# Turning the experts' operands by DRAM and VectorE instead of TensorE, in an attention and mixture-of-experts kernel

## The chip, the cores and the metric

The kernel runs on one core of one Trainium2 chip. The metric is device time in microseconds (us), the median of several executions. Engines are named as the profile names them: PE is TensorE (PEld its weight loads), DVE is VectorE, ACT is ScalarE, POOL is GpSimd, SP is SyncE, which issues most DMAs.

## The reference, cut to what matters

Eight batches of attention with a soft cap (12 heads, 448 positions, width 64), then for each batch a layer in which the 128 best scored of its 448 tokens pass through a two-layer expert.

```python
scores = scale * np.matmul(q, k.transpose(0, 1, 3, 2))
scores = cap * np.tanh(scores / cap)
scores = scores - np.max(scores, axis=-1, keepdims=True)
attn = np.exp(scores)
attn = attn / (np.sum(attn, axis=-1, keepdims=True) + 1e-09)
x = matmul(attn, v)                       # per batch (448, 768)
...
top_idx = np.argpartition(-scores[b], capacity)[:capacity]   # scores = x @ w_gate, capacity 128
xe = x[b, top_idx]
h = np.maximum(xe @ w1, 0.0)              # (128, 1024)
ye = h @ w2                               # (128, 768)
g = 1.0 / (1.0 + np.exp(-scores[b, top_idx]))
out[b, top_idx] = x[b, top_idx] + g[:, None] * ye
```

## The kernel before, in words

Attention is cut into 24 "doubles", three to a batch; a double is four heads. Each has 7 steps of 64 key positions. A step is one `qk` task (4 matmuls into `ps`), a tanh and an exp of 128x896 on ACT (`p`), and one product task (4 matmuls, `acc<-p,v`). The trace records each of these fp32 matmuls twice, so a task of 4 is 8 records. DVE adds up the exps of a double (`e<-e,p`), turns the finished accumulator in blocks of 32x32 (`xT<-acc`, once for each double, which also frees the accumulator for the next double), turns and reduces the sums (`turned`, `T`), normalises (`xn` or `room`), and weighs by the gate (`jk`, `part`). In the first three doubles part of the sums is made on PE instead (`pb<-ones,p`, 28 matmuls a group, 56 records).

After a batch's third double its tokens are scored (`quads`), ranked by way of a DRAM line (`line`, `row`), picked (a one-hot `sel`, a small matmul) and gathered from the output by an indirect DMA on POOL (`xe`, 128 tokens by 768). The expert's operands must have the feature on the partitions, so `xe` is turned by 6 PE transposes (`pb<-ident,xe`), and the first layer's result `hs` (128x1024) by 8 (`pb<-ident,hs`). ACT copies a turned piece into a high part (`xh`, `hh`), DVE subtracts it to get the low part (`xl`, `hl`), both in fp32r. A layer is then three products, high by high, high by low weight, low by high weight: 36 matmuls of 512 columns for `w1`, 48 of 384 columns for `w2`, called heavy here. DVE combines (`xe<-pb,both,xe`), POOL scatters.

Nothing is ordered by hand: functions add tasks with a duration, a priority and the buffers they take, and `Plan.run` lists them by a simulated clock, engine by engine, in which each engine then runs them in order. `WAY` holds numbers by segment of the program that steer it (when PE leaves attention for heavy work, how long it stays, how much heavy work is held for the end). The costs of tasks are in the `add` calls; `LOAD` is the planner's picture of a DMA. In `expert_tasks` the names that the change touches are `split` (transposes, high, low), `xs`, `hx`, `group`, `relu`, `combine`, `scatter` and `K.last_heavy`, the last heavy matmul so far, which the next batch's first layer waits for: one batch's two layers are finished before the next batch's start.

Of the kernel before, what the change touches and what calls it, by code (L numbers as in the profile page):

```python
# [9 lines left out]
F32 = mybir.dt.float32  # L10
# [8 lines left out]
P = 128  # L19
# [21 lines left out]
WAY = {  # L41
    "visit": (6500, 4000, 4000, 4000, 3000, 3000, 3000, 3000, 7500, 7000, 7000, 6000, 7500, 7500,
        7500, 4000, 5500, 7500, 4500, 5000, 7000, 5000, 5000, 8000),
    "enough": (2, 3, 4, 4, 4, 3, 4, 5, 3, 2, 2, 2, 1, 5, 5, 2, 1, 3, 1, 2, 1, 2, 2, 2),
    "wait": (0, 1, 0, 0, 1, 1, 1, 1, 1, 1, 0, 0, 0, 0, 0, 0, 0, 0, 0, 0, 1, 0, 1, 1),
    "eager": (0, 2, 0, 2, 0, 0, 0, 0, 0, 0, 0, 0, 0, 0, 0, 0, 0, 0, 0, 0, 0, 0, 0, 0),
    "lag": (3, 4, 4, 4, 2.5, 3, 1.5, 4, 2.5, 4, 2, 2, 4, 2, 3, 3, 2, 3, 4, 2, 1.5, 4, 3, 2.5),
    "ask": (-4, 12, -8, -4, 12, 8, -8, -12, 12, 4, -4, 4, 4, 4, 12, 12, -4, -8, -4, 8, 8, 12, 0, 0),
    "fin": (0, 4, -4, 4, -8, -8, -4, -4, 8, 14, 4, 8, 14, 14, -4, -4, -4, 0, 0, -4, -4, 8, -8, 4),
    "turn": (20, 28, 0, 28, 10, 10, 10, 10, 0, 0, 28, 28, 20, 28, 28, 10, 20, 28, -10, 20, 10, 28,  # L50
        20, 20),
    "reserve": (42000, 10000, 0, 46000, 42000, 50000, 20000, 50000, 20000, 30000, 0, 0, 0, 0, 42000,
        0, 20000, 30000, 30000, 30000, 30000, 0, 0, 0),
    "sums": (0, 0, 0, 8, 0, -2, 4, 4, 0, -4, -4, -4, 8, 8, 8, 4, 2, -4, -4, -4, 2, 2, -4, 0),
    "cast": (-20, 0, -10, -30, -30, -30, -30, -20, 20, 0, 0, 0, 20, 10, -20, 10, 10, -10, -10, 20,
        10, 20, -20, 20),
}
# [411 lines left out]
def attention_tasks(tc, K, D):  # L469
# [3 lines left out]
    if D.d == 0:  # L473
        lqk = add("NONE", 3700, lambda t: None)
        lmore = add("NONE", 750, lambda t: None, [lqk])
        lrest = add("NONE", 850, lambda t: None, [lmore])
        lv = add("SP", 0, lambda t: D.load_v(tc, K, None), prio=-19.5, load=(1, P * S * 8))
    else:
        lqk = add("SP", 0, lambda t: D.load_qk(tc, K, t.got["qk"]),
                  [K.staged[2]] if D.d == 1 else (), prio=g0 - 12, take=("qk",),  # L480
                  load=(2, P * S * 16))
        lv = add("SP", 0, lambda t: D.load_v(tc, K, t.got["v"]),
                 [lqk] if D.d == 1 else (), prio=g0 - 11, take=("v",),
                 load=(1, P * S * 8))
    pv, exps, ths, pvs, alone = None, [], [], [], []
    for s in range(NS):
# [22 lines left out]
        if g:  # L509
            a = add("PE", 754 if g > 1 else 1300, qk, [lqk if g > 1 or D.d else lmore], prio=g, take=("S",), mode="att",  # L510
                    give=[("qk", lqk)] if D.d and s == NS - 1 else ())
# [4 lines left out]
        else:  # L516
            c = S // 2
            a = add("PE", 740, lambda t, f=qk: f(t, c1=c), [lqk], prio=-2, take=("S",), mode="att")
            th = add("ACT", 510, lambda t, f=tanh: f(t, c1=c), [a], prio=-2, take=("P",))
            a2 = add("PE", 740, lambda t, f=qk: f(t, c0=c), [lmore, a], prio=-1, mode="att")  # L520
            th2 = add("ACT", 510, lambda t, f=tanh: f(t, c0=c), [a2, th], prio=-1, give=[("S", a)])
        ex_ = add("ACT", 934, exp, [th if g else th2], prio=blk + 1, seg=("lag", D.d, 2))
# [265 lines left out]
def expert_tasks(tc, K, b, s0, M, ranked, before, vals, p0):  # L788
# [30 lines left out]
    def index(t):  # L819
        nc.vector.tensor_copy(X["idx"], X["both"][:, 0:1])  # L820

    def gather(t):
# [46 lines left out]

    lows = []  # L870
    hold = add("NONE", 0, xs, [ga], prio=e0, take=("xs",))
    for i0 in range(0, ND, 3):
        w = min(3, ND - i0)
        turn, high, low = split("xe", "xh", "xl", i0, w)
        tr = add("PE", 109 * w, turn, [hold], prio=e0 - 9000, take=("bank",), mode="full")
        hi = add("ACT", 371, high, [tr], prio=-10)
        lo = add("DVE", 433, low, [hi], prio=-40 + b / 100, give=[("bank", tr)])
        lows.append(lo)

# [16 lines left out]
    hts, tail = [], None  # L896
    turned = []
    for hf in range(2):
        fs = slice(hf * 512, hf * 512 + 512)
# [22 lines left out]
    add("NONE", 0, lambda t: None, [tail], give=[("xs", hold)])  # L922
    add("NONE", 0, lambda t: None, hts, give=[("hsb", hs_owner)])
    for hf in range(2):
# [16 lines left out]
        co = add("DVE", 496, combine, [tail, g3], prio=-40 + b / 100, give=[("bank", owner)])  # L941
    K.last_heavy = tail
    add("NONE", 0, lambda t: None, [tail], give=[("hx", hh)])

    def scatter(t):
# [98 lines left out]
def main_kernel(ctx: ExitStack, tc: tile.TileContext, qk, v, cap, w_gate, w1, w2, out, C, dims):  # L1044
# [15 lines left out]
    K.weighed = {}  # L1060
    K.last_heavy = None
    K.const = ctx.enter_context(tc.tile_pool(name="const", bufs=1))
    dram = ctx.enter_context(tc.tile_pool(name="dram", bufs=1, space=bass.MemoryType.DRAM))
    K.line = [dram.tile([K.NCH * P], F32, name=f"line{i}") for i in range(2)]
    K.work = ctx.enter_context(tc.tile_pool(name="work", bufs=1))
    first = early_loads(tc, K, cap)
    with tc.manual_schedule(engines={mybir.EngineType.PE, mybir.EngineType.DVE}):
        load_flag(tc, K)
    K.psS = ctx.enter_context(tc.tile_pool(name="psS", bufs=1, space=PSUM))
    K.psV = ctx.enter_context(tc.tile_pool(name="psV", bufs=1, space=PSUM))  # L1070
    K.psB = ctx.enter_context(tc.tile_pool(name="psB", bufs=1, space=PSUM))

# [14 lines left out]
    with tc.If(fast > 0) as cmp:  # L1087
        if C <= P:
            K.plan = Plan(SIZES)
            engines = {mybir.EngineType.PE, mybir.EngineType.Activation, mybir.EngineType.DVE,  # L1090
                       mybir.EngineType.Pool, mybir.EngineType.SP}
# [78 lines left out]
```

## Time and profile before

| what | value |
|---|---|
| median of 3 executions | 447.81 us (446.86 to 449.22) |
| the profiled execution's own time | 446.97 us |
| its span, first to last instruction | 445.2 us |
| PE, DVE, ACT, POOL busy | 432.6, 376.6, 339.8, 23.8 us (97, 85, 76, 5%) |
| PE matmul records | 4600 |
| moved by DMA | 59.35 MB, mean 133 GB/s |
| granted TensorE clock | 0.998 of full speed over the span |

A busy share is the union of an engine's instructions, each from its start to its modelled end; instructions of one engine overlap by their latency, so what one costs in a full stretch is read from start to start. The 24 `xT<-acc` instructions, one per double, serve as marks: the first starts at 25.46 us, the last at 390.67 us.

### The profile page before, as it was taken

How to read it: one execution, taken by the hardware profiler on the slowest of the kernel's cores; microseconds unless marked ns; L12 is line 12 of the kernel's file. 1: busy time of each engine (PE TensorE's matmuls, PEld its weight loads, DVE VectorE, ACT ScalarE, POOL GpSimd, SP SyncE). 2: the span in 40 equal slices, each digit the busy share in tenths (PEclk: the TensorE clock that was granted, in tenths of full speed). 3: DMA queues.
4: the chain of work that ended last, by engine and by line, in shares of the span. 5: the costliest groups of instructions: out<-in, count | busy, mean ns of one | idle time of the engine just before them, and what ended most of it. 6: DMA issues, size and time to landing. Idle time of an engine off the chain costs nothing.

```text
span 445.2 us, 10844 instructions
## 1 busy us (share of the span) xinstructions
PE 432.6 (97%) x4600; PEld 247.8 (56%) x4600; DVE 376.6 (85%) x539; ACT 339.8 (76%) x395; POOL 23.8 (5%) x26
## 2 busy tenths in 40 slices
PE   8999998999999999999999999999999999999994
PEld 2455433355574455457475386554644563588984
DVE  3899999999999979999897995999969999984311
ACT  5999989999769969897769963997499989611120
POOL 3000000100002000101010010001000010000000
PEclk9999999999999999999999999999999999999999
DMA  8975753537327724453417440475244641152111
GB/s 277 346 248 174 218 153 123 160 87 197 65 93 207 195 57 135 139 170 108 144 46 231 126 102 24 150 196 159 66 141 103 191 120 43 35 125 63 35 38 40
DMA packets 46202, 59.35 MB, mean 133 GB/s; under 512 B 18242, under 2 KB 33474, under 8 KB 46146
## 3 DMA queue, kind: packets, MB, share of 16 engines
q1 hardware_dynamic: 44434, 51.83, 40.0%
q0 software_dynamic: 1280, 6.29, 4.3%
q8 instruction: 38, 0.62, 0.6%
q10 hardware_dynamic: 432, 0.46, 0.3%
q14 instruction: 18, 0.15, 0.1%
HBM read 44.40 MB, written 14.17 MB: 132 GB/s over the span
## 4 chain that ended last, share of the span: by engine, by line
PE 54%; DVE 22%; issue 10%; ACT 8%; DMA 4%; POOL 0%; POOLq 0%; SPq 0%; DVEq 0%; ACTq 0%
PE pb L887 21%; PE acc L455 15%; PE ps L447 14%; DVE e L546 9%; ACT p L498 4%; ACT p L501 3%; DVE xT L560 2%; PE pb L850 2%; DVE w2l L404 2%; DMA stage<-in_moe_w 1%; DMA xe<-out,idx 1%; DVE w1l L404 1%; DVE turned L568 1%; DVE T L572 1%; DMA room<-in_qk 1%
## 5 line engine op out<-in xcount | busy, mean ns | idle before, releaser
L498 ACT ACTIVATE p<-ps,sc 128x896 f32<-128x896 f32 (+1 forms) x169 | 165.3, 1010 | 26.7 <-PE ps L447 25.9
L501 ACT ACTIVATE p<-p,capc 128x896 f32<-128x896 f32 x168 | 170.5, 1057 | 0.6
L455 PE MATMUL acc<-p,v 64*64 64x448 f32 x1288 | 145.4, 540 | 1.6 <-DVE xT L560 1.5
L447 PE MATMUL ps<-qk 64*64 64x448 f32 x1288 | 145.5, 539 | 0.0
L546 DVE TENSOR_TENSOR e<-e,p 128x896 f32<-128x896 f32 x113 | 122.1, 1080 | 11.0 <-ACT p L501 9.8
L447 PEld LDWEIGHTS ps<-qk 64*64 64x64 f32 x1288 | 46.7, 133 | 67.0 <-issue 38.3
L455 PEld LDWEIGHTS acc<-p,v 64*64 64x64 f32 x1288 | 46.3, 133 | 63.1 <-issue 50.4
L908 ACT ACTIVATE hs<-pb 128x512 f32<-128x512 f32 x16 | 9.6, 601 | 38.8 <-PE pb L887 38.8
L546 DVE TENSOR_TENSOR e<-p 128x896 f32<-128x896 f32 x24 | 25.9, 1079 | 4.2 <-ACT p L501 4.2
L560 DVE STREAM_TRANSPOSE xT<-acc 128x896 f32<-128x896 f32 x24 | 26.4, 1099 | 3.3 <-PE acc L455 2.5
L887 PE MATMUL pb<-w2l,hh 128*128 128x384 f32 x128 | 29.1, 342 | 0.0
L887 PE MATMUL pb<-w2h,hh 128*128 128x384 f32 x128 | 28.7, 344 | 0.0
L887 PE MATMUL pb<-w2h,hl 128*128 128x384 f32 x128 | 28.1, 337 | 0.0
L887 PE MATMUL pb<-w1h,xh 128*128 128x512 f32 x96 | 27.2, 404 | 0.0
L760 DVE SCALAR_TENSOR_TENSOR jk<-row,vals,least 128x512 bf16<-128x512 f32 (+1 forms) x32 | 23.9, 747 | 3.8 <-DMA row<-line 3.1
L693 DVE TENSOR_REDUCE part<-jk 128x14 f32<-128x896 f32 x24 | 25.8, 1077 | 0.1
L887 PE MATMUL pb<-w1l,xh 128*128 128x512 f32 x96 | 25.6, 398 | 0.0
L887 PE MATMUL pb<-w1h,xl 128*128 128x512 f32 x96 | 25.5, 397 | 0.0
L568 DVE STREAM_TRANSPOSE turned<-e 128x896 f32<-128x896 f32 x21 | 23.2, 1105 | 0.3
L857 DVE TENSOR_TENSOR hl<-pb,hh 128x512 fp32r<-128x512 f32 x16 | 11.0, 684 | 14.5 <-ACT hh L854 14.4
L887 PEld LDWEIGHTS pb<-w2h,hh 128*128 128x128 f32 x128 | 22.2, 188 | 1.4 <-issue 0.7
L887 PEld LDWEIGHTS pb<-w2h,hl 128*128 128x128 f32 x128 | 22.7, 188 | 0.0
(97 smaller groups left out, 368.7 us busy)
## 6 DMA issues: line engine op xcount, KB each, us to landing
qk<-in_qk SPq DMA_DIRECT2D x46, 448.0 KB, 5.0
v<-in_v SPq DMA_DIRECT2D x23, 448.0 KB, 3.6
out<-xn SPq DMA_DIRECT2D x16, 224.0 KB, 4.3
out<-room SPq DMA_DIRECT2D x16, 224.0 KB, 4.0
stage<-in_moe_w SPq DMA_DIRECT2D x7, 384.0 KB, 3.8
stage<-in_moe_w SPq DMA_DIRECT2D x4, 512.0 KB, 4.1
out<-xn SPq DMA_DIRECT2D x16, 112.0 KB, 4.1
out<-room SPq DMA_DIRECT2D x16, 112.0 KB, 2.5
```

The source lines that it names most:

```text
L404: nc.vector.tensor_tensor(lo[:, i, :], box["st"][:, :m], hi[:, i, :].bitcast(F32), op=ALU.subtract)
L447: tc.nc.tensor.matmul(ps[HALF[r], j, c0:c1], lhsT=D.qk[r][HALF[j], at:at + HD], rhs=D.qk[r][HALF[j], 2 * HD + c0:2 * HD + c1], start=True, ...
L455: tc.nc.tensor.matmul(D.acc[HALF[j], r, :K.S], lhsT=D.v[HALF[r], s, j, :], rhs=D.P[s][HALF[r], j, :], start=(s == 0), stop=(s == K.NS - 1))
L498: nc.scalar.activation(D.P[s][:, :, c0:c1], box["ps"][:, :, c0:c1], AF.Tanh, scale=K.sc)
L501: nc.scalar.activation(D.P[s], D.P[s], AF.Exp, scale=K.cap)
L546: nc.vector.tensor_tensor(box["E"], box["E"] if n else D.P[s0], D.P[s], op=ALU.add)
L560: nc.vector.transpose(D.xT, D.acc[:, :, :S])
L568: nc.vector.transpose(box["turned"], parts[0]())
L693: nc.vector.tensor_reduce(K.part[b][:, grp, :], box["jk"], axis=AX.X, op=ALU.add)
L760: nc.vector.scalar_tensor_tensor(out=jk[:m], in0=box["row"][:m].rearrange("p (q c) -> p q c", c=NCH), scalar=score[:m, c:c + 1], in1=K.lea ...
L857: nc.vector.tensor_tensor(X[lo][:, i0:i0 + w, :M], Y["pt"][:, :w, :M], X[hi][:, i0:i0 + w, :M].bitcast(F32), op=ALU.subtract)
L887: nc.tensor.matmul(X["acc" + n_ops][:M, :ns[1]], lhsT=X[l][:, i, :M], rhs=K.wts[r][:, i, ns[2]], start=bool(start and n == 0), stop=(stop ...
```

## The change

For batches 0 to 6 the tokens, and for batches 0 to 5 the first layer's result, are no longer transposed on PE. The rows are written to a DRAM tile by an SP DMA, read back by four SP DMAs with a permuted view, so that blocks of 32x32 stand on the right partitions, and one VectorE block transpose of 128x768 or 128x1024 finishes the turn (`across`). One ACT copy and one DVE subtraction of the full width then make the parts (`parts_of`). Batch 7's tokens, and the first layer's result of batches 6 and 7, stay on PE; batch 7's tokens get one ACT copy more (`xp`), since the weights' features now stand in another order (`by_chunk`, on the host). `K.last_heavy` becomes two numbers, so that a batch's first layer waits only for the previous first layer. The last batch scatters its two halves apart. Also new: the last piece of the first `qk` load is issued later, the first step's two halves use two score buffers, `psB` is allocated first, some planner costs differ, and the whole `WAY` table is new.

```diff
-LOAD = {"issue": 440, "land": 1410, "rate": 395, "seen": 250, "lanes": 8}
+LOAD = {"issue": 440, "land": 1410, "rate": 370, "seen": 250, "lanes": 8}
+TURNED = (0, 1, 2, 3, 4, 5, 6), (0, 1, 2, 3, 4, 5)
 WAY = {
-    "visit": (6500, 4000, 4000, 4000, 3000, 3000, 3000, 3000, 7500, 7000, 7000, 6000, 7500, 7500,
+    "visit": (5500, 3500, 5500, 5500, 6500, 6500, 2500, 5500, 5500, 5500, 2000, 3000, 3000, 2000,
...
-    cuts = (0, 2 * HD + K.S // 2, 2 * HD + K.S, 2 * K.S)
+    cuts = (0, 2 * HD + K.S // 2, 2 * HD + K.S)
...
+    def across(src, n, which, deps, into, held, prio):
+        rows = K.rows[which][b % 2]
+        sent = []
+        for cols, ready in deps:
+            def out(t, cols=cols):
+                if type(cols) is slice:
+                    nc.sync.dma_start(rows[:M], X[src][:M])
+                else:
+                    at = slice(cols * P, cols * P + P)
+                    nc.sync.dma_start(rows[:M].rearrange("p (a e) -> p a e", a=4)[:, :, at],
+                                      X[src][:M].rearrange("p (a e) -> p a e", a=4)[:, :, at])
+
+            sent.append(add("SP", 0, out, [ready], prio=prio, load=(1, P * n * 4 // len(deps))))
+
+        def back(t):
+            into()
+            for a in range(4):
+                nc.sync.dma_start(
+                    X["quad"][QUAD[a]].rearrange("p (k e) -> p k e", k=4),
+                    rows.rearrange("(k i) (a e) -> a i k e", k=4, a=4)[a])
+
+        def turn(t):
+            nc.vector.transpose(X["turn"].rearrange("p c (k i) -> p k c i", k=4),
+                                X["quad"].rearrange("p (k c f) -> p k c f", k=4, f=Q))
+
+        landed = add("NONE", 0, lambda t: None, sent, prio=-100)
+        ba = add("SP", 0, back, [landed], prio=prio, take=(held,), load=(4, P * n * 4))
+        return ba, add("DVE", 30 + 1.06 * n, turn, [ba], prio=-40 + b / 100)
+
+    def parts_of(w, hi, lo, tag, ready):
+        def high(t):
+            nc.scalar.copy(X[hi], X["turn"])
+
+        def low(t):
+            X[lo] = w_tile(K, [P, w, P], F32R, *tag, lo)
+            nc.vector.tensor_tensor(X[lo], X["turn"], X[hi].bitcast(F32), op=ALU.subtract)
...
+    if turned_x:
+        hold, tr = across("xe", DM, 0, [(slice(0, DM), ga)], xq, "xs", p0)
+        lows = [parts_of(ND, "xh", "xl", ("xl", 0), tr)]
+    else:
+        hold = add("ACT", 700, xs, [ga], prio=-20, take=("xs",))
...
-                    [*lows, *K.weights["w1"], tail, K.last_heavy])
+                    [*lows, *K.weights["w1"], tail, K.last_heavy[0]])
...
+    K.last_heavy[0] = tail
+    first, tail = tail, K.last_heavy[1]
+    if turned_h:
+        hh, tr = across("hs", K.F, 1, kept, hq, "hx", p0)
+        hts = turned = [parts_of(NF, "hh", "hl", ("m", 1), tr)] * 2
...
-                        [turned[part], tail])
+                        [turned[part], tail, first])
...
+        if halves:
+            def scatter_half(t, ds_=ds_, hf=hf):
+                nc.gpsimd.indirect_dma_start(
+                    out=K.out[b].rearrange("s (t e) -> (s t) e", t=2),
...
+    for h, queue in ((1, tc.nc.scalar), (0, tc.nc.sync)):
+        queue.dma_start(first.qk[h][:, 2 * HD + K.S:], K.qk[0, h, :, 2 * HD + K.S:])
-    plan.add("SP", 3500, lambda t: None, prio=-1000)
+    plan.add("SP", 3940, lambda t: None, prio=-1000)
```

How the order of instructions moves is shown at two places. The first is PE's order before, where batch 0's tokens are turned and its first layer begins; 45 `qk` tasks stand ahead of the transposes.

```order
L590 MATMUL pb<-T,same 64x14 x4
L447 MATMUL ps<-qk 64x448 x8
L455 MATMUL acc<-p,v 64x448 x4
L447 MATMUL ps<-qk 64x448 x4
L455 MATMUL acc<-p,v 64x448 x8
L447 MATMUL ps<-qk 64x448 x8
L850 MATMUL pb<-ident,xe 128x128 x6
L455 MATMUL acc<-p,v 64x448 x8
L447 MATMUL ps<-qk 64x448 x4
L887 MATMUL pb<-w1h,xh 128x512 x6
L887 MATMUL pb<-w1l,xh 128x512 x6
L887 MATMUL pb<-w1h,xl 128x512 x6
```

In the change the same layer's first matmuls stand on PE behind 59 `qk` tasks, and nothing is transposed ahead of them.

```order
L592 MATMUL two<-T,same 64x14 x4
L450 MATMUL ps<-qk 64x448 x4
L458 MATMUL acc<-p,v 64x448 x8
L450 MATMUL ps<-qk 64x448 x4
L458 MATMUL acc<-p,v 64x448 x4
L450 MATMUL ps<-qk 64x448 x4
L458 MATMUL acc<-p,v 64x448 x4
L450 MATMUL ps<-qk 64x448 x4
L952 MATMUL pb<-w1h,xh 128x512 x6
L952 MATMUL pb<-w1l,xh 128x512 x6
L952 MATMUL pb<-w1h,xl 128x512 x6
```

The layer moved back by 13 or 14 steps of attention, and the transposes left PE. The second place is DVE's order in the change, where batch 0's tokens are turned: `xq` is what the four DMAs brought back.

```order
L548 TENSOR_TENSOR e<-e,p 128x896
L665 TENSOR_TENSOR room<-xT,rec 128x2x14x32
L892 STREAM_TRANSPOSE xt<-xq 128x4x6x32
L689 TENSOR_TENSOR jk<-room,wg 128x896
L548 TENSOR_TENSOR e<-e,p 128x896
L905 TENSOR_TENSOR xl<-xt,xh 128x768
L695 TENSOR_REDUCE part<-jk 128x14
L548 TENSOR_TENSOR e<-p 128x896
```

Before, DVE's order at the same work of attention (the weighing of batch 1's second double) holds no turn, and the two `xl` of batch 0 already stand further up.

```order
L546 TENSOR_TENSOR e<-e,p 128x896
L663 TENSOR_TENSOR room<-xT,rec 128x2x14x32
L560 STREAM_TRANSPOSE xT<-acc 128x896
L687 TENSOR_TENSOR jk<-room,wg 128x896
L546 TENSOR_TENSOR e<-e,p 128x896
L693 TENSOR_REDUCE part<-jk 128x14
L546 TENSOR_TENSOR e<-e,p 128x896
```

So a turn of 768 elements and a subtraction of 768 stand between the sums of attention, in the queue that also frees the accumulator.

## Rows read from the trace of the kernel before

**Rows 1.** Busy time of each engine, five stretches cut at the 1st, 7th, 21st, 24th xT.

```profile
core 0: us, PE busy (x) PEld busy (x) DVE busy (x) ACT busy (x) POOL busy (x), PEclk, DMA share, GB/s
0.00:25.50 25.50, 22.64 (x324) 9.27 (x325) 16.92 (x32) 20.44 (x24) 4.32 (x10) 1.00 0.86 302
25.50:106.40 80.90, 77.41 (x1178) 35.72 (x1174) 80.01 (x119) 77.30 (x86) 1.12 (x1) 1.00 0.56 167
106.40:345.80 239.40, 238.89 (x2364) 134.39 (x2356) 216.76 (x295) 196.48 (x229) 11.80 (x9) 1.00 0.45 128
345.80:390.70 44.90, 44.86 (x459) 24.74 (x452) 43.28 (x62) 37.66 (x44) 2.64 (x2) 1.00 0.32 94
390.70:445.20 54.50, 48.80 (x305) 43.65 (x303) 19.60 (x38) 7.95 (x15) 3.90 (x4) 0.99 0.23 61
```

**Rows 2.** Timeline of PE, early: start, duration, instruction.

```profile
45.02 0.93 PE L455 MATMUL acc<-p,v 64*64 64x448 f32 x8
45.77 0.96 PE L581 MATMUL pb<-ones,p 64*64 64x24 f32 x56
46.55 0.96 PE L447 MATMUL ps<-qk 64*64 64x448 f32 x8
```

**Rows 3.** Timeline of PE, late, heavy work and transposes.

```profile
418.92 0.82 PE L850 MATMUL pb<-ident,xe 128*128 128x128 f32 x6
419.49 0.94 PE L887 MATMUL pb<-w2h,hh 128*128 128x384 f32 x4
...
421.68 1.56 PE L887 MATMUL pb<-w1h,xh 128*128 128x512 f32 x6
423.08 1.56 PE L887 MATMUL pb<-w1l,xh 128*128 128x512 f32 x6
...
434.49 0.85 PE L887 MATMUL pb<-w2h,hl 128*128 128x384 f32 x4
435.18 0.85 PE L887 MATMUL pb<-w2h,hh 128*128 128x384 f32 x4
```

**Rows 4.** Timeline of DVE, early and late.

```profile
23.72 1.23 DVE L404 TENSOR_TENSOR w1l<-stage,w1h 128x1024 fp32r<-128x1024 f32 x1
24.86 0.69 DVE L401 CAST w1h<-hs 128x1024 fp32r<-128x1024 f32 x1
25.46 1.11 DVE L560 STREAM_TRANSPOSE xT<-acc 128x896 f32<-128x896 f32 x1
26.49 1.18 DVE L404 TENSOR_TENSOR w1l<-hs,w1h 128x1024 fp32r<-128x1024 f32 x1
...
390.67 1.05 DVE L560 STREAM_TRANSPOSE xT<-acc 128x896 f32<-128x896 f32 x1
391.65 1.05 DVE L687 TENSOR_TENSOR jk<-room,wg 128x896 f32<-128x896 f32 x1
...
394.61 0.55 DVE L857 TENSOR_TENSOR xl<-pb,xh 128x384 fp32r<-128x384 f32 x1
395.07 0.68 DVE L857 TENSOR_TENSOR hl<-pb,hh 128x512 fp32r<-128x512 f32 x1
```

**Rows 5.** The chain that ended last, two steps of ACT.

```profile
330.98 1.86 ACT p L501 x2
367.12 1.89 ACT p L498 x2
```

**Rows 6.** DMA issues: KB each, median us to landing.

```profile
out<-room SPq DMA_DIRECT2D x16, 112.0 KB, 2.5
row<-line SPq DMA_DIRECT2D x7, 256.0 KB, 5.3
```

**Rows 7.** Timeline of DVE and POOL, the last batch.

```profile
414.17 0.97 POOL L823 DMA_INDIRECT xe<-out,idx  x1 [9.48 <-DVE both L832]
420.01 1.02 DVE L857 TENSOR_TENSOR xl<-pb,xh 128x384 fp32r<-128x384 f32 x2 [2.36 <-ACT xh L854]
440.44 0.97 POOL L946 DMA_INDIRECT out<-xe,idx  x1 [16.68 <-DVE xe L937]
```

More of the change, by code (lines that the diff above doesn't have):

```diff
@@ L47 @@
[L47 to L53, printed above, removed]
@@ L54 @@
-    "sums": (0, 0, 0, 8, 0, -2, 4, 4, 0, -4, -4, -4, 8, 8, 8, 4, 2, -4, -4, -4, 2, 2, -4, 0),
-    "cast": (-20, 0, -10, -30, -30, -30, -30, -20, 20, 0, 0, 0, 20, 10, -20, 10, 10, -10, -10, 20,
-        10, 20, -20, 20),
+    "visit": (5500, 3500, 5500, 5500, 6500, 6500, 2500, 5500, 5500, 5500, 2000, 3000, 3000, 2000,
+        8500, 7500, 5000, 11000, 7500, 6000, 14000, 11000, 4500, 2500),
+    "enough": (1, 4, 1, 2, 2, 2, 2, 4, 2, 3, 2, 1, 2, 3, 4, 4, 3, 1, 2, 5, 3, 1, 5, 4),
+    "wait": (0, 0, 0, 0, 0, 1, 0, 1, 1, 0, 0, 1, 0, 1, 0, 0, 1, 1, 0, 1, 1, 1, 1, 0),
@@ L57 @@
+    "reserve": (42000, 50000, 20000, 30000, 80000, 38000, 42000, 54000, 60000, 0, 80000, 30000,
+        80000, 70000, 42000, 0, 42000, 54000, 10000, 0, 20000, 42000, 0, 0),
+    "sums": (8, 0, 4, 4, 2, -4, 8, 4, 2, 8, 8, 8, 8, 0, -2, -2, -4, 4, 4, 4, -2, -2, 4, 0),
+    "cast": (20, -10, 0, 0, 0, 10, -10, 20, 10, 0, 0, 20, 20, 10, -10, -10, -20, 10, 0, -30, 20, 0,
+        -30, 20),
 }
@@ L517, in attention_tasks @@
             c = S // 2
[L518 to L521, printed above, removed]
+            a = add("PE", 1030, lambda t, f=qk: f(t, c1=c), [lqk], prio=-2, take=("S",), mode="att")
+            th = add("ACT", 520, lambda t, f=tanh: f(t, c1=c), [a], prio=-2, take=("P",), give=[("S", a)])
+            a2 = add("PE", 1030, lambda t, f=qk: f(t, c0=c), [lmore, a], prio=-1, take=("S",), mode="att")
+            th2 = add("ACT", 520, lambda t, f=tanh: f(t, c0=c), [a2, th], prio=-1, give=[("S", a2)])
         ex_ = add("ACT", 934, exp, [th if g else th2], prio=blk + 1, seg=("lag", D.d, 2))
@@ L793, in expert_tasks @@
     X = {}
+    halves = b == K.B - 1
     def one_hot(t):
@@ L820, in index @@
         nc.vector.tensor_copy(X["idx"], X["both"][:, 0:1])
+        if halves:
+            X["half"] = w_tile(K, [P, 2], I32, "half", 0, "half")
+            for hf in range(2):
+                nc.vector.tensor_scalar(X["half"][:, hf:hf + 1], X["both"][:, 0:1], 2.0, float(hf),
+                                        op0=ALU.mult, op1=ALU.add)
     def gather(t):
@@ L860, in split @@
         return turn, high, low
-    def xs(t):
-        X["xh"] = w_tile(K, [P, ND, P], F32R, "xh", 0, "xh")
-        X["xl"] = w_tile(K, [P, ND, P], F32R, "xl", 0, "xl")
+    def across(src, n, which, deps, into, held, prio):
[28 more added lines that the diff above has]
+            nc.vector.tensor_tensor(X[lo], X["turn"], X[hi].bitcast(F32), op=ALU.subtract)
+        h = add("ACT", 57 + w * P / 1.2, high, [ready], prio=-10)
+        return add("DVE", 25 + 1.06 * w * P, low, [h], prio=-40 + b / 100)
+    turned_x, turned_h = (K.fast_now and b in bs and M == P for bs in TURNED)
     def hx(t):
@@ L868, in hx, with xs, xq, hq @@
         X["hl"] = w_tile(K, [P, NF, P], F32R, "m", 1, "hl")
[L870 to L878, printed above, removed]
+    def xs(t):
+        X["xp"] = w_tile(K, [P, DM], F32, "xt", 0, "xp")
+        X["xh"] = w_tile(K, [P, ND, P], F32R, "xh", 0, "xh")
+        X["xl"] = w_tile(K, [P, ND, P], F32R, "xl", 0, "xl")
+        nc.scalar.copy(X["xp"][:M].rearrange("p (c a f) -> p a c f", a=4, f=Q),
+                       X["xe"][:M].rearrange("p (a c f) -> p a c f", a=4, f=Q))
+    def xq():
+        X["quad"] = w_tile(K, [P, DM], F32, "xl", 0, "xq")
+        X["turn"] = w_tile(K, [P, ND, P], F32, "xt", 0, "xt")
+        X["xh"] = w_tile(K, [P, ND, P], F32R, "xh", 0, "xh")
+    def hq():
+        X["quad"] = w_tile(K, [P, K.F], F32, "m", 1, "hq")
+        X["turn"] = K.hs.rearrange("p (c m) -> p c m", m=P)
+        X["hh"] = w_tile(K, [P, NF, P], F32R, "m", 0, "hh")
+    if turned_x:
[3 more added lines that the diff above has]
+        hold = add("ACT", 700, xs, [ga], prio=-20, take=("xs",))
+        lows = []
+        for i0 in range(0, ND, 3):
+            turn, high, low = split("xp", "xh", "xl", i0, 3)
+            tr = add("PE", 327, turn, [hold], prio=e0 - 9000, take=("bank",), mode="full")
+            hi = add("ACT", 371, high, [tr], prio=-10)
+            lows.append(add("DVE", 433, low, [hi], prio=-40 + b / 100, give=[("bank", tr)]))
     def group(n_ops, ops, ns, start, stop, deps, bank_owner=None):
@@ L897, in expert_tasks @@
     turned = []
+    kept = []
     for hf in range(2):
@@ L949, in scatter @@
             in_=X["xe"][:M], in_offset=None)
+    if halves:
+        sc.give = [("xe", hot)]
+        return hot, sc
     return hot, add("POOL", 1250, scatter, [co], prio=p0, lat=3600, give=[("xe", hot)])
@@ L1064, in main_kernel @@
     K.line = [dram.tile([K.NCH * P], F32, name=f"line{i}") for i in range(2)]
+    K.rows = [[dram.tile([P, n], F32, name=f"rows{n}_{i}") for i in range(2)] for n in (K.DM, K.F)]
     K.work = ctx.enter_context(tc.tile_pool(name="work", bufs=1))
@@ L1068, in main_kernel @@
         load_flag(tc, K)
+    K.psB = ctx.enter_context(tc.tile_pool(name="psB", bufs=1, space=PSUM))
     K.psS = ctx.enter_context(tc.tile_pool(name="psS", bufs=1, space=PSUM))
     K.psV = ctx.enter_context(tc.tile_pool(name="psV", bufs=1, space=PSUM))
-    K.psB = ctx.enter_context(tc.tile_pool(name="psB", bufs=1, space=PSUM))
     def bank(i):
```

57 lines of the change are left out of this document (39 added, 18 removed).

## The prediction

> **What bounds the kernel now.** I cut the span at four of the 24 xT starts and read each engine's busy time between them [rows 1]. Up to the 7th xT three engines are nearly full: of 80.9 us PE has 77.41, DVE 80.01, ACT 77.30. From the 7th to the 24th PE is never free (238.89 of 239.40, then 44.86 of 44.90), while DVE has 22.6 us to spare in the long stretch (216.76). After the 24th, PE works off the last two batches' experts almost alone. The granted clock is 1.00 until the last stretch (0.99), so it carries no term. PE time removed therefore shortens the span only as far as DVE and ACT can follow, and the change puts work on DVE.
>
> **Paces.** From start to start: four attention matmuls 0.75 us, a group of 28 sums on PE 0.78 [rows 2]; a PE transpose 0.095 (six in 0.57), a w1 matmul 0.233 (six in 1.40), a w2 matmul 0.173 (four in 0.69) [rows 3]. DVE: a 128x896 operation 0.98 to 1.03, a 1024-wide subtraction 1.14, a 1024-wide cast 0.60, xl from PSUM 0.46 for 384 [rows 4]; hl for 512 by its width 0.61. ACT: 0.93 an exp, up to 0.95 a tanh [rows 5].
>
> **What is removed.** 42 transposes of tokens and 48 of first-layer results leave PE: 90 x 0.095 = 8.6 us. PE goes from attention to heavy work and back 41 times instead of 45; I put 0.2 us on a passage, an estimate between nothing and half a task of attention (0.38), so 0.8. In all PE loses 9.3 us. Next to each other in one heavy visit, transposes cost nothing more.
>
> **What is added on DVE.** No block transpose of 768 or 1024 stands in the trace of before; by width from the 896 of xT it is 0.88 and 1.18. A batch's tokens take 0.88 plus one 768-wide subtraction (0.86, three quarters of 1.14) in place of two xl (0.92): +0.8. A first layer's result takes 1.18 + 1.14 in place of two hl (1.2): +1.1. Seven and six times, that is 12.3 us. [...] ACT copies the same widths in one piece as before in two: no term.
>
> **What is added in DMA.** One or two writes and four reads for each turn, 384 or 512 KB each way. The nearest rows are 2.5 us from issue to landing for the 112 KB stores, 5.3 for the broadcast row read [rows 6], so a way takes some 5 to 11 us, where six PE transposes took 0.57. Behind a write that waits for its gather stand, on SP, loads of qk and v two doubles ahead; a double lasts 15 us (365 us over 23), so a delay of some us is covered. If that cover were gone, PE would wait for a qk load by the excess. What the way's length does cost is the first batch: its first layer stands behind 59 qk tasks instead of 45, so attention has to run alone for longer, at DVE's and ACT's pace.
>
> Here a rule speaks against the change. A PE transpose of 128 columns takes 0.095 us of PE, a DVE turn 0.147 of DVE (0.88 over six) plus the way [rows 3, 4]; per 128x128 the change pays more engine time than it frees. The Trainium skill, VectorE: DVE Perf Modes, section Rules for kernel authors, says to transpose 128x128 on TensorE where a PSUM result will do, and keeps VectorE for 32x32 blocks within a bank. By its table in The three transpose paths (390 ns against 311 ns, bf16) 90 turns would free 35 us of PE and cost 28 of DVE, an estimate and with 28 in place of the 13.2 that the turns take by the rows the sum below would be 15 us higher, 460. The rows of this fp32 kernel do not bear that out: the turns of before run at 0.147 for 128 columns.
>
> **The sum, stretch by stretch**, by counting the changed order's instructions between the same xT:
> - To the 1st xT: two sum groups (1.56) and one qk task (0.75) fewer ahead of it: 25.5 - 2.3 = 23.2. The later issue of the last qk piece and the second score buffer of the first step I take as nothing: the first step's work is covered by ACT's chain of tanh and exp; without that cover 0.5 us either way.
> - 1st to 7th: PE has two sum groups and four qk tasks more, but 20 w1 matmuls and 6 transposes fewer: 1.6 us less. DVE has two pairs of w1 casts more (3.5), less a sum, a w2 subtraction and two xl (2.8): +0.6. ACT has 42 exps and 45 tanhs: 79 us at 0.9. So 80.9 + 0.5 = 81.4, bound by ACT and DVE, and PE waits for 7 us of it.
> - 7th to 21st: PE loses 64 transposes (6.1), 60 w2 (10.4), two qk tasks (1.5) and gains 20 w1 (4.7); with small ones -14.0: 225.4. DVE gets nine turns (9.2), and with single subtractions for pairs, four sums, one T, one w2 subtraction more and two combines fewer (the rest) +12.6 in all: 229.4 by busy time. Counted at paces from start to start, it is 225.6 against 213.0 before. DVE is now the longer one. I take the middle, 227.6.
> - 21st to 24th: PE gains 60 w2 (10.4) and 10 w1 (2.3), loses 10 transposes and a qk task: +11.4, 56.3. DVE (43.28 + 1.8) is not in the way.
> - After the 24th: PE loses 10 transposes and 10 w1, with one passage more: -2.8. But before, 12 w2 matmuls lay between the last tokens' transposes and their first layer (419.49 to 421.68) and hid the high and low parts, which end at 421.03 [rows 3, 7]; now that layer stands right behind them and waits 1.5 us. Further, from the 24th xT to the last tokens' transposes took 28.2 us (390.67 to 418.92); the changed order puts 0.7 us more of DVE into that chain, and 0.8 of ACT for xp (by the width of a tanh), and leaves PE 28.1 us of other work to fill it: 1.5 us of waiting. The smaller last scatter gives back 0 to 1.8 (half of the time from 440.44 + 0.97 to the end): I take 0.4, since a small DMA's landing still costs most of it. 54.5 - 2.8 + 3.0 - 0.4 = 54.3.
>
> Sum 23.2 + 81.4 + 227.6 + 56.3 + 54.3 = 442.8 against 445.2: 2.4 us less. The profiled execution took 446.97, so 444.6 on the same footing; the median of the runs shown is 0.84 above it, so **445.4 us**. Half a per cent, about what a measurement of this kernel can tell from no change, is 2.2 us.
>
> **The rivals.**
> - *All of PE's saving arrives.* DVE's idle time of before, 22.6 us in the long stretch, is enough if its order fits. For it: 12.6 is less than 22.6. Against: the same stretch must also be 14 us shorter. 9.3 - 2.6 (what PE waits more at the end) = 6.7 us less: 441.1.
> - *DVE's order binds double by double.* xT frees the accumulator, so a double that is heavy on DVE can't borrow from the next. Taking the largest load for pairs of doubles from the 7th to the 21st gives 33.1, 31.7, 27.8, 30.8, 29.6, 30.4, 47.6 = 231.0 (before, 237.3 by the same count, measured 239.4): 233 instead of 227.6, so **slower**, 450.8. It decides once the alternation costs over 2.4 us more than I took. The Trainium skill's rule above would end here, and this chance is all that the traces give it.
> - *The way lands late.* The turns stand in DVE's in-order queue ahead of attention's sums. Each us by which a landing comes after its place stops DVE; 13 turns at 0.5 us are 6.5: 451.9. For it: 5.3 us for the row read. Against: DVE itself runs late where it binds, and then the data has landed.
>
> **How the numbers follow.** The forecast has 0.40, all of the saving 0.28, DVE double by double 0.18, late landings 0.14. Around the forecast +-2.5 us half lies beyond 0.5% on the fast side. Faster 0.28 + 0.16 = 0.44; same 0.21 of the forecast + 0.07 of milder forms of the two slow rivals = 0.28; slower the rest of these, with 0.03 of the forecast: 0.28. The range leaves out the strongest forms of both sides: 439.5 to 451.5.
>
> **What would show it.** 22 PE transposes of tokens and results instead of 112; DVE busy some 389 us, over 96% between the 7th and the 21st xT, and PE with idle time there, put down to DVE or ACT; the first w1 matmul near 110 us. If DVE's waits name the DMA of xq or hq for several us, late landings are right. If PE stays over 99% from the 7th xT on, the first rival is. Wrong altogether would be a turn that takes more than 1.5 us.

## The result and the profile after

The changed kernel takes 452.86 us (median of 4, 452.4 to 455.45) against 447.51 of the kernel before beside it: a ratio of 1.0125, 95% interval 1.0077 to 1.0174. It is slower, by 1.25%, and above the range of the prediction. The profiled execution has a span of 450.6 us, 5.4 more than before.

The busy windows of the changed kernel, cut at the same four xT starts as [rows 1]:

```profile
core 0: us, PE busy (x) PEld busy (x) DVE busy (x) ACT busy (x) POOL busy (x), PEclk, DMA share, GB/s
0.00:21.80 21.80, 18.79 (x152) 6.56 (x156) 13.39 (x27) 17.77 (x21) 4.32 (x10) 1.00 0.90 317
21.80:105.30 83.50, 77.80 (x1316) 35.04 (x1308) 80.60 (x118) 79.88 (x88) 1.30 (x1) 1.00 0.60 181
105.30:337.90 232.60, 227.29 (x2224) 121.37 (x2228) 225.23 (x296) 198.90 (x222) 8.71 (x7) 1.00 0.58 163
337.90:397.10 59.20, 57.39 (x536) 36.17 (x529) 45.83 (x64) 36.38 (x41) 4.35 (x4) 1.00 0.50 140
397.10:450.60 53.50, 45.87 (x292) 40.79 (x290) 21.03 (x40) 7.69 (x13) 4.86 (x5) 0.98 0.19 54
```

Against the forecast of 23.2, 81.4, 227.6, 56.3 and 54.3 the stretches are off by -1.4, +2.1, +5.0, +2.9 and -0.8: 7.8 us in all. PE, never free from the 7th to the 24th xT before, now has 5.3 us of idle time in the long stretch and 1.8 in the next; DVE fills 96.8% of the long one.

The turns themselves, grouped by shape (durations min/median/max in ns):

```profile
L892 DVE STREAM_TRANSPOSE xt<-xq x7: 968/972/979, 108.5 to 393.0; 128x768 f32<-128x768 f32 x7
L892 DVE STREAM_TRANSPOSE hs<-hq x6: 1235/1245/1246, 130.8 to 400.3; 128x1024 f32<-128x1024 f32 x6
L905 DVE TENSOR_TENSOR hl<-hs,hh x6: 1215/1218/1224, 133.6 to 402.8; 128x1024 fp32r<-128x1024 f32 x6
```

These are as costed: from start to start a turn takes some 0.90 and 1.17 us (0.88 and 1.18 were put in). What waits, on DVE and then on PE (in total, times, longest):

```profile
DVE xe L1016 <- PE pb L952: 17.4, 7, 3.5
DVE hl L865 <- ACT hh L862: 10.4, 3, 5.5
DVE e L548 <- ACT p L503: 10.1, 8, 4.1
DVE hs L892 <- DMA hq<-rows: 3.5, 2, 1.8
```

```profile
PE ps L450 <- ACT p L500: 3.9, 6, 1.2
PE acc L458 <- DVE xT L562: 2.7, 4, 1.5
PE two L810 <- DVE sel L801: 2.5, 3, 1.7
PE two L592 <- DVE T L574: 2.3, 3, 1.3
```

DVE waits for the way (the write to DRAM and the reads back) only twice for a first layer's result (3.5 us) and once for tokens (0.6). That looks like little. The timelines of DVE, PE and SP at one of the two places show what it does:

```profile
337.37 1.21 SPq L879 DMA_DIRECT2D rows<-hs  x2
...
346.24 0.86 PE L952 MATMUL pb<-w2h,hl 128*128 128x384 f32 x4
...
347.13 3.83 SPq L887 DMA_DIRECT2D hq<-rows  x4
...
351.93 1.09 DVE L548 TENSOR_TENSOR e<-e,p 128x896 f32<-128x896 f32 x1 [4.10 <-ACT p L503]
354.72 1.25 DVE L892 STREAM_TRANSPOSE hs<-hq 128x1024 f32<-128x1024 f32 x1 [1.70 <-DMA hq<-rows]
355.89 0.65 DVE L801 SCALAR_TENSOR_TENSOR sel<-iota,rk 128x512 f32<-128x512 f32 x1
...
356.69 0.64 PE L810 MATMUL two<-vals,sel 64*64 64x2 f32 x32 [1.68 <-DVE sel L801]
```

SP issues the four reads over 3.83 us. DVE has just waited 4.10 us for an exp, so it comes early to the turn and stops there for 1.70 us; the one-hot stands behind the turn, and PE waits 1.68 us for the one-hot. No slack lies between: the late landing reaches PE whole.

It wasn't a slow transfer that made this landing late. The rows had been written from 337.37 us on, and from 344 to 348 us the DMA engines moved nothing (DMA share 0.00, the last but one figure):

```profile
344.00:348.00 4.00, 4.00 (x42) 3.37 (x45) 0.76 (x3) 0.00 (x0) 0.00 (x0) 1.00 0.00 0
```

The reads start at 347.13 us, right behind the last `w2h,hl` matmul of the batch before (346.24 + 0.86 = 347.10). `hq` has the place in SBUF that held that batch's `hl`, and the reads wait on PE until it has been read. At the other place, the turn at 215.8 us, the DMA engines were full instead (share 1.03 from 208 to 212 us, 0.87 in the next 4).

### The profile page after: what moved, and what is told of

It reads as the page before. It is cut to its first block, busy times and chain, and to the rows that moved or that the text cites. A ratio compares the mean times of both kernels' runs of the same rounds, so it can differ in the third digit from the quotient of the medians.

```text
span 450.6 us, 10750 instructions
## 1 busy us (share of the span) xinstructions
PE 427.1 (95%) x4510; PEld 239.9 (53%) x4510; DVE 386.1 (86%) x541; ACT 340.6 (76%) x383; POOL 23.5 (5%) x27
## 4 chain that ended last, share of the span: by engine, by line
PE 44%; DVE 28%; DMA 11%; issue 6%; ACT 6%; SPq 4%; POOLq 0%; DVEq 0%; ACTq 0%
PE pb L952 20%; PE ps L450 12%; DVE e L548 11%; PE acc L458 10%; DMA hq<-rows 5%; ACT p L500 3%; DVE jk L762 3%; ACT p L503 2%; SPq L887 2%; DVE xT L562 2%; DMA rows<-xe 1%; DVE w2l L407 1%; DVE turned L570 1%; DVE part L695 1%; DVE jk L689 1%
## 5 line engine op out<-in xcount | busy, mean ns | idle before, releaser
L952 PE MATMUL pb<-w1h,xh 128*128 128x512 f32 x96 | 26.0, 402 | 0.2 <-ACT xh L862 0.2
L1016 DVE SCALAR_TENSOR_TENSOR xe<-pb,both,xe 128x384 f32<-128x384 f32 x16 | 9.8, 610 | 17.4 <-PE pb L952 17.4
```

The costliest lines, as they stand in the source:

```text
L952: nc.tensor.matmul(X["acc" + n_ops][:M, :ns[1]], lhsT=X[l][:, i, :M], rhs=K.wts[r][:, i, ns[2]], start=bool(start and n == 0), stop=(stop ...
L1016: nc.vector.scalar_tensor_tensor(out=X["xe"][:M, ds_], in0=X["acc" + nm][:M, :HH], scalar=X["gt"][:M], in1=X["xe"][:M, ds_], op0=ALU.mult, ...
```

## Experiments

"Idle time of PE" below is the span less PE's busy time: 445.2 - 432.6 = 12.6 us before, 450.6 - 427.1 = 23.5 after. So PE was busy 5.5 us less and idle 10.9 us more. The expectations name larger figures (30.5 us for the changed kernel); they set PE's work by the paces of [rows 2] and [rows 3] and an estimate for the passages, and compare only with each other. A span is that of the one profiled execution, whose time can lie up to 2.2 us from its run's median; so the medians' differences stand beside the spans'. Theory A: VectorE's added work delays what PE waits for. Rival B: the way lands late. Rival C: the planner, whose VectorE durations are 2 to 16% below the trace, made an order that is wrong for a full VectorE. Each time is compared with the kernel before beside it, at 447.5 to 448.7 us.

**Shorter turns.** The order of every engine is kept.

```diff
-            nc.vector.transpose(X["turn"].rearrange("p c (k i) -> p k c i", k=4),
-                                X["quad"].rearrange("p (k c f) -> p k c f", k=4, f=Q))
+            nc.vector.transpose(X["turn"].rearrange("p c (k i) -> p k c i", k=4)[:, :, :1],
+                                X["quad"].rearrange("p (k c f) -> p k c f", k=4, f=Q)[:, :, :1])
```

> The changed kernel with every VectorE turn cut to its first block column (32 elements of 192 or 256 per quarter, so a sixth or an eighth of the width); the rest of the turned operand keeps old data, so part of the turning is left out. Every engine's order and every DMA stay as in the changed kernel. VectorE's load falls by 7 x 0.75 + 6 x 1.05 = some 11.5 us. Theory A (VectorE is too full, and TensorE waits for its late results): some 6 to 9 us less than the changed kernel's 452.9, so 444 to 447. Theory B (the new order itself, with its later first layers, leaves TensorE idle whatever VectorE does): within 2 us of 452.9.

447.39 us, ratio 0.9971 (0.9946 to 0.9996); span 446.4. Of some 11.5 us taken from DVE 4.2 arrive in the span, 5.5 in the median. A part of the cause, not all.

**The low subtractions cut as well** (`X[lo][:, :1]`, in the same way).

> The kernel of the run with short turns (447.4 us), with each turned result's low subtraction on VectorE cut to its first block column as well (13 subtractions of 0.87 and 1.14 us, some 13 us of VectorE in all on top of the 11.5 already gone); the order of every engine is the changed kernel's. It leaves out part of the turning and of the low parts. If the fullness of VectorE is what makes TensorE wait, each us taken from VectorE between the 7th and the 24th xT gives back up to half a us, as the first cut did (4.2 of 11.5): 440 to 444 us, TensorE idle 18 to 22 us. If the order itself holds TensorE idle whatever VectorE's load is: within 2 us of 447.4, TensorE idle still over 25 us.

445.09 us, 0.9938 (0.9918 to 0.9959); span 442.6, idle time of PE 17.5 us. Another 3.8 us of span, 2.3 of the median. Both cuts together, some 24.5 us of DVE, give 8.0 us of span and 7.8 of the median: each us of DVE is worth about a third of one.

**No turns, and tokens alone turned**, with the changed kernel's table of numbers.

```diff
-TURNED = (0, 1, 2, 3, 4, 5, 6), (0, 1, 2, 3, 4, 5)
+TURNED = (), ()
```

> The changed kernel with no batch turned by the way (all 48 and 64 transposes on TensorE again), the new table and everything else as changed. VectorE loses 12.3 us, TensorE gets 9.3 us. Theory A: 446 to 449, as the kernel before. Theory B (the new table and order cost the time): 452 or more, since the table stays.

> The changed kernel with only the tokens turned by the way (7 batches), the first layer's results by TensorE (64 transposes), the rest as changed. VectorE loses 6.6 us against the changed kernel, TensorE gets 4.6. Theory A: about halfway back, 448 to 451. Theory B: 452 or more. If the first layer's way (two writes, four reads, and a whole first layer to wait for) is what costs, 446 to 448.

464.49 us (1.0348, 1.0292 to 1.0405) and 471.98 (1.0507, 1.0456 to 1.0557). Inconclusive. By their numbers both fit the second reading (452 or more), but in both PE waits over 6 us at one place for the last batch's tokens (`xp`), and in the second 7.0 more for an `xh`. The table steers another list of tasks, so these say nothing of the turning.

**The low subtraction on GpSimd** (`nc.gpsimd.tensor_tensor` in `low`).

> The changed kernel with the low parts of the turned operands subtracted on GpSimd instead of VectorE, emitted at the same place; the order on every other engine stays. VectorE's load falls by 7 x 0.87 + 6 x 1.14 = 12.9 us, and GpSimd, 5% busy, takes 13 operations of some 1 to 3 us each. Theory A: 443 to 447, unless GpSimd takes over 3 us an operation, when the second layers start late. Theory B: within 2 us of 452.9.

456.59 us, 1.0161 (1.011 to 1.0213). DVE was hardly relieved (385.3 us busy, 386.1 in the changed kernel): see the last section.

**Corrected durations, a table searched anew,** for the changed kernel, for the same without turns, and for the kernel before (`PACED` maps the planner's VectorE costs to the trace's).

```diff
+PACED = {970: 1000, 992: 1031, 971: 995, 680: 755, 576: 602, 496: 528, 433: 464, 570: 600, 56: 60,
+         208: 242, 844: 896, 1115: 1169, 839: 868, 1110: 1137, 430: 467, 573: 602}
...
+            if t.eng == "DVE":
+                t.ns = PACED.get(int(t.ns), t.ns)
```

> The changed kernel with the planner's VectorE durations set to what the trace shows (4 to 11 per cent longer: xT 1.00 for 0.97, rank 0.755 for 0.68, a turn 0.896 for 0.844 and so on) and its order table searched anew for these; the turning itself is unchanged. If the order for a too fast VectorE is the cause of the lost time: 439 to 444 us, faster than the kernel before by over 0.8 per cent, and TensorE idle of 18 to 24 us in place of 30.5. If the turning's load on VectorE is the cause whatever the order: 449 to 453.

> The changed kernel with no batch turned by the way (both sets empty, so tokens and first-layer results go through TensorE as before), everything else of the change kept, with the same corrected VectorE durations and a table searched anew as long as for the turned one. With this and the turned one the tables are equally fit, so their difference is what the turning is worth. If the turning is worth what TensorE loses: 3 to 7 us above the turned one. If VectorE's load eats it: within 2 us of the turned one, or below it.

> The kernel before with the corrected VectorE durations and a table searched anew. If the corrected durations and the search give time back in any order, it comes to 440 to 444 us, faster than the kernel before by about one per cent: then what the change was measured against is not the best of its own kind either. If VectorE's spare time made the wrong durations harmless there: within 0.5 per cent of the kernel before, 445 to 449.

453.05 us (1.0096, 1.0062 to 1.0131), 449.15 (1.0044, 1.0025 to 1.0063) and 446.5 (0.9969, 0.9954 to 0.9984). The new order did not mend the turned kernel, so C as stated falls. With tables searched equally long, turning costs 3.9 us (453.05 against 449.15), as the reading has it in which VectorE's load eats the gain. The kernel with the rest of the change and no turns is in turn 2.7 us slower than the kernel before with a new table; it copies the tokens of all batches once more on ACT (347.5 us busy against 339.6), and no run separates that from the new order and the pairing of batches. PE idles 13.5 and 13.1 us in the two kernels without turns, 26.3 with them. And now the landings are the longest waits behind DVE's usual ones, as the waits of the turned kernel with the new table show:

```profile
DVE xt L899 <- DMA xq<-rows: 6.3, 4, 3.3
DVE hs L899 <- DMA hq<-rows: 6.0, 4, 2.0
```

**Turns that wait for no landing**, in the order of the changed kernel and in the new one. The way's reads go to DRAM, the turn reads a resident weight.

```diff
-                                X["quad"].rearrange("p (k c f) -> p k c f", k=4, f=Q))
+                                K.wts["w1h"][:, 0, :n].bitcast(F32).rearrange(
+                                    "p (k c f) -> p k c f", k=4, f=Q))
...
-        X["quad"] = w_tile(K, [P, K.F], F32, "m", 1, "hq")
+        X["quad"] = K.land[1][b % 2]
```

> The changed kernel in its own order; all writes and reads of the way run, but the reads land in DRAM and a turn takes its data from a resident weight, so that no turn waits for a landing. VectorE's work is the same. It leaves out the real turning. If waits for the way hold a part of the lost time: VectorE's 4.1 us of waiting for it disappear, and the time falls by 2 to 4 us from 452.9, to 449 to 451. If the fullness of VectorE alone does it: 452 to 453.5, no change.

> The same edit in the order searched anew for the true VectorE durations (453.05 us, in which VectorE waited 12.3 us for the way, and its turns came up to 11 us behind their place in the plan). If the way's length, which the planner has shorter than the traces show, is what undid the new order: it falls by 6 to 10 us, to 443 to 447. If VectorE's load undid it: less than 2 us, still over 451.

448.23 us (0.9994, 0.9979 to 1.001) and 445.6 (0.9937, 0.9921 to 0.9953). In the changed order the 4.1 us of waiting are worth 3.8 us of span (446.8), 4.6 of the median; in the new order 12.3 us are worth 9.0 (452.8 to 443.8), 7.5 of the median. The reads also have a place of their own here, so the wait for the place of `hl` goes together with the wait for the landing, and these runs don't tell the two apart. Here are the long stretch and the next of the changed order without landings (same columns as above); beside 232.60 and 59.20 they lose 1.3 and 1.8 us:

```profile
104.90:336.20 231.30, 226.47 (x2224) 121.77 (x2228) 225.03 (x296) 198.83 (x222) 8.70 (x7) 1.00 0.56 164
336.20:393.60 57.40, 57.27 (x536) 36.15 (x529) 45.72 (x64) 36.19 (x41) 4.36 (x4) 1.00 0.51 148
```

**Neither the turns' work nor the landings** (both edits).

> The changed kernel in its own order with both suspects taken away together: turns cut to their first block column (11.5 us of VectorE) and reading a resident weight, so that none waits for a landing. It leaves out the turning. Alone, the cut gave 4.2 us of span and the missing landings 3.8. If these are two separate losses they add up: span 441 to 444 from 450.6, time 444 to 446. If both are one loss (a late turn holds up a full VectorE, and a shorter turn makes it up): span 445 to 447, no better than either alone. If they hold each other up it comes below 441.

444.88 us (0.993, 0.9905 to 0.9955), span 442.3: together 8.3 us of span, near the sum of the two (4.2 and 3.8). By the medians it is 8.0 us against 5.5 and 4.6, so the two may overlap by some 2 us, which is within the spread of the changed kernel's four executions (452.4 to 455.45). A and B are two losses, and neither stands for the other; that they add up in full is shown by the spans alone.

**The load alone and the way alone, in the kernel before.** Thirteen block transposes that nobody needs; and thirteen ways that nobody waits for.

```diff
+            if i0 and M == P and b < (6 if src == "hs" else 7):
+                n = K.F if src == "hs" else DM
+                nc.vector.transpose(X[src][:, :n].rearrange("p (c k i) -> p k c i", k=4, i=Q),
+                                    K.wts["w1h"][:, 0, :n].bitcast(F32).rearrange(
+                                        "p (k c f) -> p k c f", k=4, f=Q))
```

```diff
...
+                nc.sync.dma_start(rows, K.wts["w1h"][:, 0, :n].bitcast(F32))
+                for a in range(4):
+                    nc.sync.dma_start(
+                        land[QUAD[a]].rearrange("p (k e) -> p k e", k=4),
+                        rows.rearrange("(k i) (a e) -> a i k e", k=4, a=4)[a])
```

> The kernel before in its own order, with 13 block transposes added on VectorE (768 wide behind seven batches' last token subtraction, 1024 wide behind six first layers' last), which read a resident weight and nobody needs: 13.3 us of VectorE, no way, no wait, TensorE's work as before. They overwrite a tile that the combination adds to, so the output is not the reference's. If VectorE's load alone delays TensorE at some 0.35 us for each us, as the cut turns and subtractions of the changed order gave it back: 451 to 454 (448 plus 4 to 6). If the order of before has room for it: under 449.5.

> The kernel before in its own order with the way's DMAs alone added behind the same low subtractions: 13 writes of a resident weight's rows to DRAM (whole, not in halves) and 52 reads of them into another DRAM tile; nobody waits for them but SP's queue. VectorE and TensorE have the work of before. The output is the reference's. If the transfers' traffic and SP's queue cost by themselves (later loads of qk and v): 450 or more, 2 us or more above before. If the way costs only through the turn that waits for it: within 1.5 us of before.

456.19 us (1.0158, 1.0131 to 1.0186) for the load, 458.21 (1.0216, 1.0174 to 1.0258) for the way. With the load, the time between the 1st and the 24th xT grows from 365.2 us to 371.0: 5.8 us, close to half of what DVE was given. Of the other 3.3 us of span 3.2 lie in the tail, about half of them the tail's granted clock (last section). With the way it grows by 0.8 only (366.0), but the tail is 8.9 us longer and holds one stop of 6.5 us on PE, put down to `sel`. SP's timeline ahead of it:

```profile
399.23 0.50 SPq L862 DMA_DIRECT2D rows<-w1h  x1
402.20 2.47 SPq L864 DMA_DIRECT2D land<-rows  x4
404.72 0.59 SPq L862 DMA_DIRECT2D rows<-w1h  x1
407.91 2.45 SPq L864 DMA_DIRECT2D land<-rows  x4
410.47 0.54 SPq L751 DMA_DIRECT2D line<-vals  x1
413.78 0.33 SPq L755 DMA_DIRECT2D row<-line  x1
```

The reads wait in SP's queue for their write to land, and the last batch's ranking row stands behind two ways; DVE waits 11.1 us for it. Between the marks, then, the traffic costs under 1 us, and the place in SP's queue 6.5 in the tail. Behind that stop PE's granted clock was 0.50 and 0.79 in the next two stretches of 4 us, up to 2.8 us more. The first xT came 1.6 us later than before, ahead of any way, and is not the way's doing.

**The way planned longer.** The new order with 1 us more for each write and each read of a way in the plan (`lat=1000`), and the table searched for that.

> The changed kernel with the corrected VectorE durations and, in addition, each write and each read of the way planned 1 us longer; its order table searched anew for these. The turning is the real one. If the two short figures (VectorE's durations and the way's length) are the whole of what the change lost, the order now keeps the data ahead of the turns: VectorE waits under 3 us for the way, and the time is near that of the same kernel whose turns wait for nothing, 444 to 447 us (445.6). If the way cannot be hidden while VectorE is full: 449 to 453, with VectorE waiting 4 us or more for it. Either way a time of 446 or more means that turning gains nothing over the kernel before with its own order searched anew (446.5).

452.7 us (1.009, 1.0059 to 1.0121), span 451.0: not mended. Up to 3.2 us of this are a fall of the granted clock (last section); without them, too, it would be above the 444 to 447 of the first reading. Landings cost DVE 3.3 us, 2.79 of them at one turn. SP's and DVE's timelines there:

```profile
178.59 0.53 SPq L880 DMA_DIRECT2D rows<-hs  x1
179.20 1.07 SPq L430 DMA_DIRECT2D qk<-in_qk  x2
180.92 3.65 SPq L681 DMA_DIRECT2D out<-room  x4
184.67 3.11 SPq L888 DMA_DIRECT2D hq<-rows  x4
192.81 1.25 DVE L893 STREAM_TRANSPOSE hs<-hq 128x1024 f32<-128x1024 f32 x1 [2.79 <-DMA hq<-rows]
```

And two windows between the write and the turn:

```profile
184.00:188.00 4.00, 4.00 (x48) 1.43 (x40) 3.90 (x8) 3.57 (x5) 0.97 (x1) 1.00 1.03 262
188.00:192.00 4.00, 4.00 (x48) 1.52 (x45) 2.02 (x3) 3.89 (x5) 0.00 (x0) 1.00 0.97 270
```

Two `qk` loads and four stores stand between the write and the reads, the DMA engines are full (share 0.97 to 1.03), and the second half's write and the turn are 14.2 us apart. One longer figure for every way doesn't cover that. Elsewhere in this run the way took 5.9 us from its write to its last landing (361.6 to 367.5).

## Why the prediction was wrong

- **The failing step of the sum: "I take the middle, 227.6."** It lets DVE borrow across doubles. Measured: 232.6, and 231.3 with the landings taken out. The count by pairs of doubles gave 231.0, and that rival's 233 is 232.6 as measured. The trace bears the rival out pair by pair. It counted 33.1, 31.7, 27.8, 30.8, 29.6, 30.4 and 47.6; here are the changed kernel's windows, cut at every second xT (columns as above):

```profile
105.30:138.00 32.70, 31.80 (x298) 16.26 (x299) 32.59 (x44) 28.00 (x32) 0.00 (x0) 1.00 0.47 141
138.00:170.20 32.20, 31.11 (x334) 16.99 (x334) 31.48 (x42) 27.22 (x31) 2.54 (x2) 1.00 0.64 178
170.20:197.60 27.40, 27.03 (x293) 12.96 (x292) 27.26 (x39) 25.67 (x30) 0.98 (x1) 1.00 0.62 176
197.60:230.20 32.60, 31.64 (x300) 15.59 (x294) 30.62 (x41) 31.09 (x36) 0.00 (x0) 1.00 0.58 157
230.20:259.60 29.40, 28.56 (x298) 13.76 (x297) 29.36 (x37) 28.61 (x32) 0.00 (x0) 1.00 0.55 148
259.60:290.70 31.10, 30.41 (x308) 16.37 (x307) 29.65 (x41) 24.88 (x29) 2.64 (x2) 1.00 0.74 205
290.70:337.90 47.20, 46.74 (x408) 29.44 (x410) 44.26 (x60) 33.43 (x39) 2.55 (x2) 1.00 0.49 146
```

In the first, third and fifth pair DVE is busy for all but 0.04 to 0.14 us; in the last PE is, but for 0.46. Only the fourth is far off its count, by 1.8 us; it holds the late landing at 215.8 us and takes 30.6 us without landings. That VectorE's load moves PE without any way is shown by the kernel before with the load added (5.8 us) and the two runs with less of it (4.2 and 3.8 us of span).
- **The way: wrong in its length and above all in what it meets.** Of 5 to 11 us forecast, the three ways that stopped DVE took 11.5, 12.7 and 16.7 from their last write's start to the turn. "If that cover were gone, PE would wait for a qk load by the excess" looked at the loads. The price lay with the turn: "DVE itself runs late where it binds, and then the data has landed" was the argument against the late landings, and it fails where DVE has just waited for something else (the 4.10 us ahead of the 1.70 shown above). The rival priced 13 late turns at 0.5 us; there were three, of 4.1 us in all, worth 3.8 us of span.
- **21st to 24th: 56.3 forecast, 59.2 measured,** 57.4 without landings. DVE "is not in the way" by its busy time (45.83 of 59.20), but one landing there stopped PE for 1.68 us.
- **PE's saving: right as far as it can be read.** 22 transposes are left of 112, as planned, 8.6 us at their pace; the passages' 0.8 us was an estimate and no run shows it. Busy time, in which every instruction counts to its modelled end, fell by 5.5 us.
- **The turns' cost: right,** within 0.02 us each, and so is DVE's busy time (386.1, some 389 forecast). Start and tail were 1.4 and 0.8 us better than forecast.
- **Slips in the sum.** The items named for the 21st to the 24th give +11.0 and not +11.4, those after the 24th -3.1 and not -2.8: 0.7 us less in all, which makes the miss larger.

So two rivals of the slow side, given 0.18 and 0.14, came together. The landings make 3.8 of the 7.8 us missed; the long stretch without them 3.7 (231.3 for 227.6); the rest, +1.6, +1.1, -1.3 and -1.1, nearly cancels. They had been treated as alternatives, although both act in the same queue. The reading that a DVE with nothing to spare can't make up a late landing fits this, but no run shows it by itself.

The advice to transpose 128x128 on TensorE (the Trainium skill, VectorE: DVE Perf Modes, section Rules for kernel authors) agrees with the result here. The estimate from its table (section The three transpose paths, for bf16) does not: at 0.90 and 1.17 us the thirteen turns cost 13.3 us, as the rows of before said (13.2), and not 28.

Whether some order makes the turning pay stays open, and so does what the rest of the change, without the turns, costs. With the landings taken away the new order reached a ratio of 0.9937; the kernel before with its own table searched anew reached 0.9969, and is the fastest version run that leaves nothing out. The searches were not all equally long, so small differences among these orders mean little. The pairing of two batches' layers was not run by itself.

## What to carry to other kernels

An engine's spare time over a stretch is not spare time at the place of the edit: count by the piece after which a buffer or a result is handed over, here two doubles, and let the larger count stand where the queue is in order. Work moved off the busiest engine to one that is nearly as full can come back as waits; here PE was busy 5.5 us less and idle 10.9 us more. A round trip through DRAM in an in-order queue needs cover at its longest, behind the loads and stores that share its queue and the last reader of the place that it lands in, not at its median.

## What the hardware showed that was not expected

**VectorE stops while GpSimd works on two operands.** With the low subtraction on GpSimd, the timelines of GpSimd and DVE:

```profile
132.59 2.70 POOL L905 TENSOR_TENSOR hl<-hs,hh 128x1024 fp32r<-128x1024 f32 x1 [19.92 <-ACT hh L901]
133.10 2.74 DVE L762 SCALAR_TENSOR_TENSOR jk<-row,vals,least 128x512 bf16<-128x512 f32 x1
135.88 0.75 DVE L762 SCALAR_TENSOR_TENSOR jk<-row,vals,least 128x512 bf16<-128x512 f32 x1
401.11 2.03 POOL L905 TENSOR_TENSOR xl<-xt,xh 128x768 fp32r<-128x768 f32 x1 [16.33 <-ACT xh L901]
401.43 1.12 DVE L562 STREAM_TRANSPOSE xT<-acc 128x896 f32<-128x896 f32 x1
402.47 1.07 DVE L570 STREAM_TRANSPOSE turned<-e 128x896 f32<-128x896 f32 x1
```

The operation with several inputs that begins inside GpSimd's ends only after it, 2.74 us for 0.75; the two transposes that begin inside the second one are not held (1.12 and 1.07); they read one tensor each, `acc` in PSUM and `e` in SBUF. The Trainium skill, SBUF — State Buffer, section SBUF: two separate sides, says that a VectorE operation with two SBUF inputs and a GpSimd operation that reads SBUF exclude each other for a whole instruction; the trace agrees. So the 13 subtractions given to GpSimd here freed only 0.8 us of VectorE's busy time.

**The clock fell after a pause of PE.** In the order with the way planned longer, PE's granted clock fell to 0.50, that is 1.2 GHz, after a stretch in which PE was busy 3.35 of 6 us; the windows there:

```profile
390.00:396.00 6.00, 3.35 (x28) 1.25 (x20) 5.75 (x6) 1.88 (x3) 0.00 (x0) 0.96 0.88 212
396.00:400.00 4.00, 2.70 (x14) 2.21 (x15) 3.97 (x6) 1.05 (x1) 0.00 (x0) 0.50 0.02 7
400.00:404.00 4.00, 4.00 (x15) 3.30 (x14) 3.19 (x5) 0.60 (x1) 0.00 (x0) 0.70 0.53 115
```

At 0.50 and 0.70 these 8 us hold up to 3.2 us of lost clock. The kernel before with the load shows the same in its tail (0.60 in a window of 4 us after 2.37 of 4 busy, 1.6 us), so that these 1.6 of its 9.1 us of span are not VectorE's doing directly. The changed kernel's last stretch keeps 0.98.
